# Row constants split over two engines, one batch masked straight from PSUM, and a later start for the second batch's attention

## The chip, the cores and the metric

One Trainium2 core runs the whole program. The metric is the device time of one execution in microseconds (us), as a median over runs.

## What is computed

Three layers in a row over 4 batches of 576 tokens. The first is attention with 8 heads of 64, in which a score stays only if it lies within `tau` of its row's largest:

```python
scores = scale * q @ k.T
thresh = max(scores, -1) - tau
scores = where(scores >= thresh, scores, -1e9)
attn = exp(scores - max) / (sum + 1e-9);  x = attn @ v      # (2304, 512)
h = x @ moe_w_in                                            # (2304, 2048)
g = (a0 + a1 h + a2 h^2 + a3 h^3) / (1 + |b0||h| + |b1| h^2 + 1e-6)
x = g @ moe_w_out                                           # (2304, 512)
h = x @ moe2_w_in
g = where(h >= 1, h, where(h <= -1, 0, (h + 1)^2 / 4))
out = g @ moe2_w_out
```

## The kernel before

The program calls the layer with the rational function MoE1 and the one with the quadratic MoE2. Values are split into a high and a low fp16 part, so that each product of two matrices takes three fp16 products.

**Attention.** A batch has four head pairs, each with nine rows, 36 rows in all. A row is 128 queries (or the last 64 of both heads) against 576 keys. For a row TensorE (PE) makes the scores in a PSUM tile (`scores`), VectorE (DVE) copies them to an SBUF tile `sc` and takes their maximum `mx` in the same instruction (L406), one DVE instruction makes two numbers of each query from `mx`, `nt[:, 0:1]` the threshold and `nt[:, 1:2]` the bias of the exponential (L407), ScalarE (ACT) makes the exponential `e` (L367), DVE masks it against the threshold (L368), ACT and GpSimd (POOL) split it into `hl` (L376 to L378), a DMA transposes that to `eT` (L380), and PE multiplies with `v` (L393). `con` holds the constants of a pair. In batch 0 the rows use two PSUM tiles in turn, tag "s" and the tag "acc" that belongs to the MoE later; in the other batches "s" alone. `prep_v` and `prep_pair` load and split a batch's v and a pair's q and k.

**MoE.** Each of the layers takes 24 steps a batch: three blocks of 192 tokens by eight chunks of 256 hidden columns. A step is a first product (`ph`, L636), the function on DVE, ACT and POOL, and a second product into `acc` (L650).

**Weights.** They come as doubles. A half chunk is loaded as words into a tile with the tag "rw" (two buffers, L219), put together to fp32 by three DVE instructions (L206 to L208), scaled by its power of two and split. MoE1's 16 halves are made beside batch 0's attention, MoE2's 16 halves beside MoE1 of batch 0. The v of batches 1 to 3 is loaded into the same "rw" buffers (L282, L284). After its last half, a maximum over all chunks (`f_max`, L238) is taken, on which the constants of MoE2 hang.

**Order.** A list scheduler sets the order of instructions on each engine from priorities (`at`). The program is written as 192 MoE steps; `spread` puts the pieces of a later batch's attention beside the steps of a range (`ATTENTION`), and the weights' halves beside steps 0 to 20 (`WEIGHTS`). Engines work their queues in order. SP issues all DMAs in one order too, and an issue whose data or buffer isn't ready holds up those behind it.

Of the kernel before, what the change touches and what calls it, by code (L numbers as in the profile page):

```python
# [9 lines left out]
F32 = mybir.dt.float32  # L10
I32 = mybir.dt.int32
AF = mybir.ActivationFunctionType
ALU = mybir.AluOpType
AX = mybir.AxisListType
# [5 lines left out]
LARGEST = 3e38  # L20
LEAST = 2.0**-60
TOP = 2.0**14
LN_E = 6.931471805599453
# [5 lines left out]
N_TEMP, N_POLY, N_WT, N_WH, N_GG, N_ROW, N_SC = 5, 3, 3, 2, 4, 3, 2  # L29


ATTENTION = {1: (14, 50), 2: (60, 100), 3: (108, 147)}
WEIGHTS = (0, 20)


# [1 line left out]
def tile_attention_moe_moe2(  # L37
# [18 lines left out]
    V, A, G, T, Q = nc.vector, nc.scalar, nc.gpsimd, nc.tensor, nc.sync  # L56
    B, H, S, D = q.shape
    P = 128
# [19 lines left out]
    ap = ctx.enter_context(tc.tile_pool(name="ap", bufs=2))  # L78
    xp = ctx.enter_context(tc.tile_pool(name="xp", bufs=1))
    mp = ctx.enter_context(tc.tile_pool(name="mp", bufs=2))  # L80
    sp = ctx.enter_context(tc.tile_pool(name="sp", bufs=4))
# [9 lines left out]
    def small(n, name, keep=False):  # L91
        if keep:
            return cp.tile([P, n], F32, name=name)
        tag = "".join(x for x in name if x.isalpha() or x == "_").rstrip("_")
        return sp.tile([P, n], F32, name=name, tag=f"s{n}_{tag}", bufs=4 if tag in ("mx", "nt") else 2)
# [12 lines left out]
    tau8, tlow = small(1, "tau8", True), small(1, "tlow", True)  # L108
# [22 lines left out]
    V.tensor_scalar(lc[:, 0:1], babs[:, 1:2], LEAST, None, op0=ALU.max)  # L131
    G.memset(lc[:, 1:2], 1.0 + 1e-6)
    A.activation(lc[:, 2:3], lc[:, 0:1], AF.Ln)
    V.tensor_scalar(pc, a_t, binv[:, 1:2], -1.0, op0=ALU.mult, op1=ALU.mult)

    def power(name, src, n, keep=False):


        f, s = small(n, name + "_f", keep), small(n, name + "_s", keep)
        V.tensor_scalar(f, src, 1.0 / TOP, TINY / TOP, op0=ALU.mult, op1=ALU.max)  # L140
        V.tensor_scalar(f.bitcast(I32), f.bitcast(I32), 0x7F800000, None, op0=ALU.bitwise_and)
        V.reciprocal(s, f)
        return f, s

    def root(name, f, src, n=1, even=False):


        s = small(n, name + "_s")
        V.tensor_scalar(f.bitcast(I32), src.bitcast(I32), 1, 0x3F000000 if even else 0x3F800000,
                        op0=ALU.logical_shift_right, op1=ALU.bitwise_and)  # L150
        top = TOP / 2 if even else TOP
        V.tensor_scalar(f, f, 2.0**96 / top, (2.0 if even else 1.0) * TINY / top, op0=ALU.mult, op1=ALU.max)
        V.reciprocal(s, f)
        return s
# [5 lines left out]
    def everywhere(name, src, n, keep=False, place=None):  # L160


        r = small(n, name, keep)
        if place is None:
            place = ps_1.tile([P, 512], F32, name="pm" + name, tag="aux")
        pm = place[:, 0 : n * P].rearrange("p (n q) -> p n q", n=n)
        for i in range(n):
            T.matmul(pm[:, i], src[:, i : i + 1].to_broadcast([P, P]), ident, start=True, stop=True)
        V.tensor_reduce(r, pm, axis=AX.X, op=ALU.max)
        return r  # L170
# [15 lines left out]
    def split(hi, lo, src, scale=None, on_vector=True):  # L186

        if scale is None:
            A.copy(hi, src)  # L189
            G.tensor_tensor(lo, src, hi, op=ALU.subtract)  # L190
        elif on_vector:
            A.activation(hi, src, AF.Copy, scale=scale)
            V.scalar_tensor_tensor(lo, src, scale, hi, op0=ALU.mult, op1=ALU.subtract)
        else:
            A.activation(src, src, AF.Copy, scale=scale)
            split(hi, lo, src)
# [68 lines left out]
    def whole(x):  # L265
        return x[..., 0 : NT * P, :].rearrange("h (p t) d -> p h (t d)", t=NT)
# [34 lines left out]
    def prep_pair(b, pr, on_vector):  # L301
        raws = rp.tile([P, 2, C + 1, D], F32, name=f"rqk{b}_{pr}", tag="rqk", bufs=1)
        raw = raws[:, :, 0:C, :]
        for x, src in enumerate((q, k)):
            Q.dma_start(raws[:, x].rearrange("p (a c) d -> p a (c d)", a=2)[:, :, 0 : NT * D],
                        whole(src[b, 2 * pr : 2 * pr + 2]))
            for ab in range(2):
                Q.dma_start(raw[ab * ST : (ab + 1) * ST, x, NT, :], src[b, 2 * pr + ab, NT * P :, :])
        mx = small(2, f"mqk{b}_{pr}")
        qk = ap.tile([P, 2, C, 2 * D], F16, name=f"qk{b}_{pr}", tag="qk", bufs=1)  # L310
        if b == 0:
            for x in range(2):
                A.activation(qk[:, x, :, 0:D], raw[:, x], AF.Square, scale=2.0**-32, accum_out=mx[:, x : x + 1])
            f = small(2, f"qkf{b}_{pr}")
            s = root(f"qkr{b}_{pr}", f, everywhere(f"mqke{b}_{pr}", mx, 2), 2)
        else:
            V.tensor_reduce(mx, raw.rearrange("p x c d -> p x (c d)"), axis=AX.X, op=ALU.max, apply_absolute_value=True)
            f, s = power(f"qk{b}_{pr}", everywhere(f"mqke{b}_{pr}", mx, 2), 2)

        con = sp.tile([P, 5], F32, name=f"con{b}_{pr}", tag="con", bufs=3)  # L320
        G.memset(con[:, 1:2], 1.0)
        G.memset(con[:, 4:5], LN_E)
        V.scalar_tensor_tensor(con[:, 0:1], f[:, 0:1], cflag, f[:, 1:2], op0=ALU.mult, op1=ALU.mult)
        V.tensor_scalar(con[:, 2:3], con[:, 0:1], -1.0, None, op0=ALU.mult)
        V.scalar_tensor_tensor(con[:, 3:4], s[:, 0:1], tau8, s[:, 1:2], op0=ALU.mult, op1=ALU.mult)
        V.tensor_tensor(con[:, 3:4], con[:, 3:4], tlow, op=ALU.min)
        for x in range(2):
            split(qk[:, x, :, 0:D], qk[:, x, :, D : 2 * D], raw[:, x], s[:, x : x + 1], on_vector)
        qkT = ap.tile([P, 2 * C, P], F16, name=f"qkT{b}_{pr}", tag="qkT")
        Q.dma_start_transpose(out=qkT, in_=qk.rearrange("p x c d -> p (x c d)"))  # L330
        kT2 = ap.tile([P, C, P], F16, name=f"kT2{b}_{pr}", tag="kT2")
        Q.dma_start(kT2[0:D], qkT[D : 2 * D, C : 2 * C, :])
        Q.dma_start(kT2[D : 2 * D], qkT[0:D, C : 2 * C, :])
        return con, qkT, kT2
# [48 lines left out]
    def weighted(pv, rows, eT, cols, vv, h, ab):  # L383

        his, los = [(c, c) for c in range(NT)], [(NT + 1 + c, c) for c in range(NT)]
        if ab:
            his, los = los, his
        blocks = []
        for c, x in [(NT, NT)] + his:
            blocks += [(c, x, 0, D + 1), (c, x, D + 1, D)]  # L390
        blocks += [(c, x, 0, D + 1) for c, x in los]
        for n, (c, x, at, w) in enumerate(blocks):
            T.matmul(pv[rows, 0:w], eT[:, c, cols], vv[:, h * NT + x if x < NT else H * NT + h, at : at + w], start=(n == 0), stop=(n == len(blocks) - 1))  # L393

    def att_rows(b, pr, g, data, pvs):

        con, qkT, kT2, vv, h = data
        name = f"{b}_{pr}_{g}"
        rows = ROWS[3 * g : 3 * g + 3]
        for r, (t, ab) in enumerate(rows):  # L400
            other = b == 0 and r % 2 == 1
            banks = ps_2.tile([P, 1024], F32, name=f"s{name}_{r}", tag="acc" if other else "s")
            scores(banks, t, ab, qkT, kT2)
            mx, nt = small(1, f"mx{name}_{r}"), small(2, f"nt{name}_{r}")
            s = ap.tile([P, S], F32, name=f"sc{name}_{r}", tag="sc", bufs=N_SC)
            V.tensor_scalar(s, banks[:, 0:S], 1.0, -LARGEST, op0=ALU.mult, op1=ALU.max, accum_out=mx)  # L406
            V.scalar_tensor_tensor(nt, con[:, 1:3], mx, con[:, 3:5], op0=ALU.mult, op1=ALU.add)  # L407
            eT = softmax(b, s, ab, con, nt[:, 1:2], nt[:, 0:1], f"{name}_{r}")
            if ab == 0:
                pv = ps_1.tile([P, 512], F32, name=f"pv{b}_{pr}_{t}", tag="ph" if b == 0 else "pv", bufs=2 if b == 0 else 1)  # L410
                pvs[t] = pv[:, 0 : 2 * (2 * D + 2)].rearrange("p (a d) -> p a d", a=2)
            if t < NT:
                weighted(pvs[t][:, ab], slice(0, P), eT, slice(0, P), vv, h + ab, ab)
            else:
                for i in range(2):
                    c = slice(i * ST, (i + 1) * ST)
                    weighted(pvs[t][:, 0], c, eT, c, vv, h + i, 0)
            if ab == 1 or t == NT:
                normalize(b, pr, t, pvs.pop(t))
# [257 lines left out]

    for b, (first, last) in ATTENTION.items():
        spread(first, last, [("att", b)] * N_UNITS)
# [71 lines left out]
```

## Time and profile before

| | us |
|---|---|
| median of three runs | 1337.6 (1337.43 to 1340.25) |
| the profiled execution's own time | 1340.14 |
| its span in the profile | 1338.3 |
| attention of batch 0 and MoE1's weights | 0 to 226.3 |
| MoE1 of batch 0, until its last second product | 226.3 to 389.4 |
| until the first second product of MoE2 | 389.4 to 461.7 |
| MoE2 of batch 0 from there on | 461.7 to 601.8 |
| MoE1 and MoE2 of batch 1 | 605.0 to 871.7 |
| MoE2 of batch 3, the last stage | 1248.1 to 1331.5 |

The stages are cut at the first and last matmuls of L636 and L650 in the trace. An engine's busy share is over the whole span and mixes stages that have different limits. The granted TensorE clock is 0.893 of full on average.

### The profile page before, as it was taken

Reading aid. Unit: us, or ns where it says so; the run is one execution under the profiler, and the core shown is the slowest. Engines: PE = TensorE matmul, PEld = TensorE weight load, DVE = VectorE, ACT = ScalarE, POOL = GpSimd, SP = SyncE. Lnnn points to the kernel's source line nnn. Section 1 sums busy time; section 2 is a strip of 40 time slices with the busy share of each in tenths; the row PEclk is TensorE's granted clock in tenths of the full one; section 3 lists DMA queues with packets and bytes.
Section 4 is the critical chain, followed back from the end, with each engine's and each line's share of the span. In section 5 each row is a group of like instructions: output and inputs, shape, how many; then the busy total and the mean of one; then the engine's idle time right before and its main releaser. Section 6 shows DMA issues by size and latency. Waiting matters only on the chain.

```text
span 1338.3 us, 31403 instructions
## 1 busy us (share of the span) xinstructions
PE 1055.2 (79%) x12498; PEld 962.3 (72%) x12498; DVE 1078.3 (81%) x2497; ACT 796.2 (59%) x1371; POOL 514.2 (38%) x572
## 2 busy tenths in 40 slices
PE   1454355577854589999888999999788998999998
PEld 0233234477752488889877888898778887999998
DVE  6896786899989968778999886889997876898421
ACT  4766554577755546657666565677665565776332
POOL 2764643344324435531135444421353453222221
PEclk9656555798985699999989999999999999999999
DMA  6878785423569737491359564922586539305100
GB/s 200 231 184 209 179 237 162 157 96 111 190 197 257 184 69 126 102 249 45 84 142 217 118 110 73 259 81 45 143 203 131 93 72 240 100 2 184 70 13 25
DMA packets 260275, 187.12 MB, mean 140 GB/s; under 512 B 220960, under 2 KB 233248, under 8 KB 251936
## 3 DMA queue, kind: packets, MB, share of 16 engines
q1 hardware_dynamic: 260128, 185.12, 54.3%
q8 instruction: 98, 1.61, 0.5%
q14 instruction: 49, 0.40, 0.1%
HBM read 106.96 MB, written 21.50 MB: 96 GB/s over the span
## 4 chain that ended last, share of the span: by engine, by line
PE 31%; DVE 28%; DMA 13%; issue 11%; POOL 7%; ACT 6%; SPq 2%; ACTq 0%; DVEq 0%; POOLq 0%
PE acc L650 14%; PE ph L636 13%; DMA eT<-hl 8%; POOL hl L378 4%; DVE e L368 4%; DMA qkT<-qk 3%; DVE sc L406 3%; PE pv L393 2%; DVE wt L207 2%; DVE t L530 2%; DVE t L529 2%; DVE t L523 2%; DVE nt L407 1%; DVE t L528 1%; DVE wt L208 1%
## 5 line engine op out<-in xcount | busy, mean ns | idle before, releaser
L650 PE MATMUL acc<-gg,wc 128*128 128x192 f16 x4608 | 426.2, 247 | 11.4 <-POOL gg L190 6.1
L636 PEld LDWEIGHTS <-wc 128*128 128x128 f16 x4608 | 392.9, 100 | 43.8 <-DVE t L525 24.7
L650 PEld LDWEIGHTS <-wc 128*128 128x128 f16 x4608 | 384.5, 98 | 13.4 <-issue 11.5
L190 POOL TENSOR_TENSOR gg<-t,gg 128x384 f16<-128x384 f32 x192 | 195.1, 1017 | 468.4 <-ACT gg L189 392.8
L636 PE MATMUL ph<-xT,wc 128*128 128x192 f16 x2304 | 221.9, 255 | 32.5 <-DVE t L525 31.1
L636 PE MATMUL ph<-yT,wc 128*128 128x192 f16 x2304 | 219.2, 247 | 2.5 <-DVE t L583 1.9
L378 POOL TENSOR_TENSOR hl<-e,hl 128x512 f16<-128x512 f32 x144 | 177.0, 1229 | 0.0
L367 ACT ACTIVATE e<-sc,nt,con 128x576 f32<-128x576 f32 x144 | 124.0, 865 | 74.5 <-DVE nt L407 62.6
L368 DVE SCALAR_TENSOR_TENSOR e<-sc,nt,e 128x576 f32<-128x576 f32 x144 | 134.7, 936 | 41.0 <-ACT e L367 40.6
L393 PE MATMUL pv<-v,eT 128*128 128x65 f16 (+1 forms) x2240 | 107.0, 207 | 73.8 <-DMA eT<-hl 58.7
L393 PEld LDWEIGHTS <-eT 128*128 128x128 f16 (+1 forms) x2240 | 96.8, 110 | 90.7 <-DMA eT<-hl 68.9
L189 ACT CAST gg<-t 128x384 f16<-128x384 f32 x192 | 97.2, 508 | 90.5 <-DVE t L583 48.2
L357 PE MATMUL s<-qkT 128*128 128x512 f16 (+3 forms) x320 | 95.7, 331 | 65.8 <-DVE sc L406 47.0
L376 ACT CAST hl<-e 128x576 f16<-128x576 f32 x144 | 96.4, 670 | 81.1 <-DVE e L368 66.5
L377 POOL TENSOR_TENSOR hl<-e,hl 128x64 f16<-128x64 f32 x144 | 57.9, 402 | 222.6 <-ACT hl L376 198.6
L582 DVE SCALAR_TENSOR_TENSOR t<-t,c 128x384 f32<-128x384 f32 x96 | 68.7, 716 | 67.2 <-ACT t L581 67.1
L406 DVE TENSOR_SCALAR_CACHE_REDUCE sc<-s 128x576 f32<-128x576 f32 x144 | 107.5, 747 | 14.1 <-PE s L358 13.2
L526 ACT ACTIVATE t<-t,lc 128x384 f32<-128x384 f32 x96 | 67.9, 708 | 44.4 <-DVE t L523 44.1
L521 ACT ACTIVATE t<-ph,sc 128x384 f32<-128x384 f32 x96 | 55.3, 576 | 64.1 <-PE ph L636 63.9
L581 ACT ACTIVATE t<-ph,c 128x384 f32<-128x384 f32 x96 | 63.9, 667 | 47.1 <-PE ph L636 45.3
L358 PEld LDWEIGHTS <-qkT 128*128 128x128 f16 (+1 forms) x320 | 32.3, 111 | 73.3 <-issue 54.5
L358 PE MATMUL s<-kT,qkT 128*128 128x512 f16 (+2 forms) x320 | 76.6, 330 | 5.4 <-DMA kT<-qkT 5.3
(169 smaller groups left out, 1556.2 us busy)
## 6 DMA issues: line engine op xcount, KB each, us to landing
wc<-scratch SPq DMA_DIRECT2D x56, 1024.0 KB, 5.8
rw<-in_moe_w_in_dram SPq DMA_DIRECT2D x16, 1024.0 KB, 5.7
rw<-in_moe_w_out_dram SPq DMA_DIRECT2D x16, 1024.0 KB, 5.4
scratch<-wc SPq DMA_DIRECT2D x8, 1024.0 KB, 5.1
scratch<-wh SPq DMA_DIRECT2D x16, 512.0 KB, 2.9
kT<-qkT SPq DMA_DIRECT2D x32, 144.0 KB, 2.5
rqk<-in_q_dram SPq DMA_DIRECT2D x16, 256.0 KB, 3.1
rqk<-in_k_dram SPq DMA_DIRECT2D x16, 256.0 KB, 3.0
```

What stands on the lines that cost most here:

```text
L189: A.copy(hi, src)
L190: G.tensor_tensor(lo, src, hi, op=ALU.subtract)
L357: T.matmul(s[rows, at : at + w], qkT[:, c, cols], k1[:, k0 : k0 + w], start=True, stop=False)
L358: T.matmul(s[rows, at : at + w], qkT[:, c, cols], k2[:, k0 : k0 + w], start=False, stop=True)
L367: A.activation(e, s, AF.Exp, bias=nb, scale=con[:, 0:1])
L368: V.scalar_tensor_tensor(e, s, th, e, op0=ALU.is_ge, op1=ALU.mult)
L376: A.copy(hi, e)
L378: G.tensor_tensor(lo_w, e[:, whole], hi[:, whole], op=ALU.subtract)
L393: T.matmul(pv[rows, 0:w], eT[:, c, cols], vv[:, h * NT + x if x < NT else H * NT + h, at : at + w], start=(n == 0), stop=(n == len(blocks) ...
L406: V.tensor_scalar(s, banks[:, 0:S], 1.0, -LARGEST, op0=ALU.mult, op1=ALU.max, accum_out=mx)
L636: last = T.matmul(ph[:, f, :], w[:, wx, kt, f * P : (f + 1) * P], rhs, start=(n == 0), stop=(n == 3 * KT - 1))
L650: T.matmul(dst, w[:, wx, f, d * P : (d + 1) * P], gg[:, gx, f, :], start=(i == 0 and f == 0 and n == 0 and d % 2 == 0), stop=(i == NCH - 1 ...
```

## The change

Three edits. First, `con` loses its two fixed columns; the bias becomes an ACT instruction of 128x1 (Identity, with a scale and a bias from SBUF), and the threshold a DVE `tensor_scalar` of 128x1. Second, in batch 0 the scores are not copied: DVE takes their maximum by a reduction, and the exponential and the mask read PSUM. Third, the 17 pieces of batch 1's attention are spread over steps 18 to 50 and no longer 14 to 50.

```diff
-ATTENTION = {1: (14, 50), 2: (60, 100), 3: (108, 147)}
+ATTENTION = {1: (18, 50), 2: (60, 100), 3: (108, 147)}
...
+    ln_e = small(1, "ln_e", True)
+    G.memset(ln_e, LN_E)
...
-        con = sp.tile([P, 5], F32, name=f"con{b}_{pr}", tag="con", bufs=3)
-        G.memset(con[:, 1:2], 1.0)
-        G.memset(con[:, 4:5], LN_E)
+        con = sp.tile([P, 3], F32, name=f"con{b}_{pr}", tag="con", bufs=3)
...
-            s = ap.tile([P, S], F32, name=f"sc{name}_{r}", tag="sc", bufs=N_SC)
-            V.tensor_scalar(s, banks[:, 0:S], 1.0, -LARGEST, op0=ALU.mult, op1=ALU.max, accum_out=mx)
-            V.scalar_tensor_tensor(nt, con[:, 1:3], mx, con[:, 3:5], op0=ALU.mult, op1=ALU.add)
+            if b == 0:
+                s = banks[:, 0:S]
+                V.tensor_reduce(mx, s, axis=AX.X, op=ALU.max)
+            else:
+                s = ap.tile([P, S], F32, name=f"sc{name}_{r}", tag="sc", bufs=N_SC)
+                V.tensor_scalar(s, banks[:, 0:S], 1.0, -LARGEST, op0=ALU.mult, op1=ALU.max, accum_out=mx)
+            A.activation(nt[:, 1:2], mx, AF.Identity, bias=ln_e, scale=con[:, 1:2])
+            V.tensor_scalar(nt[:, 0:1], mx, con[:, 2:3], None, op0=ALU.add)
```

How the order moves is shown at two places. Line numbers of the changed kernel are 2 higher from L131 to L319, the same from L323 to L404, and 5 higher behind the change in `att_rows`. There L407 is batch 0's maximum, L411 the bias on ACT, L412 the threshold, and L368 the mask still.

On DVE, in the second group of rows of batch 0's first pair (names end in pair, group and row, and in a number of their own), weights and norms in between left out, before:

```order
L407 SCALAR_TENSOR_TENSOR nt0_0_1_0_481<-con0_0_162,mx0_0_1_0_480 128x2
L406 TENSOR_SCALAR sc0_0_1_1_526,mx0_0_1_1_524<-s0_0_1_1_519 128x576
L407 SCALAR_TENSOR_TENSOR nt0_0_1_1_525<-con0_0_162,mx0_0_1_1_524 128x2
L368 SCALAR_TENSOR_TENSOR e0_0_1_0_485<-sc0_0_1_0_482,nt0_0_1_0_481,e0_0_1_0_485 128x576
L406 TENSOR_SCALAR sc0_0_1_2_560,mx0_0_1_2_558<-s0_0_1_2_553 128x576
L407 SCALAR_TENSOR_TENSOR nt0_0_1_2_559<-con0_0_162,mx0_0_1_2_558 128x2
L368 SCALAR_TENSOR_TENSOR e0_0_1_1_529<-sc0_0_1_1_526,nt0_0_1_1_525,e0_0_1_1_529 128x576
L406 TENSOR_SCALAR sc0_0_2_0_690,mx0_0_2_0_688<-s0_0_2_0_683 128x576
L407 SCALAR_TENSOR_TENSOR nt0_0_2_0_689<-con0_0_162,mx0_0_2_0_688 128x2
L368 SCALAR_TENSOR_TENSOR e0_0_1_2_563<-sc0_0_1_2_560,nt0_0_1_2_559,e0_0_1_2_563 128x576
```

and now:

```order
L407 TENSOR_REDUCE mx0_0_1_0_478<-s0_0_1_0_473 128x1
L407 TENSOR_REDUCE mx0_0_1_1_522<-s0_0_1_1_517 128x1
L412 TENSOR_SCALAR nt0_0_1_0_479<-mx0_0_1_0_478,con0_0_164 128x1
L412 TENSOR_SCALAR nt0_0_1_1_523<-mx0_0_1_1_522,con0_0_164 128x1
L368 SCALAR_TENSOR_TENSOR e0_0_1_0_483<-s0_0_1_0_473,nt0_0_1_0_479,e0_0_1_0_483 128x576
L368 SCALAR_TENSOR_TENSOR e0_0_1_1_527<-s0_0_1_1_517,nt0_0_1_1_523,e0_0_1_1_527 128x576
L407 TENSOR_REDUCE mx0_0_1_2_556<-s0_0_1_2_551 128x1
```

Before, the copy of a row came ahead of the mask of the row before it, and needed only an `sc` buffer. Now two maxima and two thresholds come first, then two masks, and the maximum of the next row comes behind the mask that gives its PSUM tile back. On ACT the two biases stand ahead of the two exponentials, and the exponentials read `s`:

```order
L411 ACTIVATE nt0_0_1_0_479<-mx0_0_1_0_478,ln_e_121,con0_0_164 128x1
L411 ACTIVATE nt0_0_1_1_523<-mx0_0_1_1_522,ln_e_121,con0_0_164 128x1
L367 ACTIVATE e0_0_1_0_483<-s0_0_1_0_473,nt0_0_1_0_479,con0_0_164 128x576
L367 ACTIVATE e0_0_1_1_527<-s0_0_1_1_517,nt0_0_1_1_523,con0_0_164 128x576
```

No bias waits for DVE's threshold, and both take their row's `mx` alone.

The second place is SP's queue at the end of MoE1 of batch 0, where the last three halves of MoE2's weights (`rw1_6_1`, `rw1_7_0`, `rw1_7_1`) and batch 1's v (`rv1_0`, `rv1_1`) take turns on the "rw" buffers, before (loads of chunks, and of q and k, left out):

```order
L256 DMA wc1_2_4188<-scratch1_123 128x4096
L284 DMA rv1_0_3600<-in_v_dram 128x8x256
L282 DMA rv1_1_3603<-in_v_dram 64x8x64 x2
L249 DMA scratch1_123<-wh1_5_0_3244 128x2048
L330 DMA_TRANSPOSE qkT1_0_3445<-qk1_0_3422 128x18x128
L219 DMA rw1_6_1_3631<-in_moe2_w_out_dram 128x2x1024
L219 DMA rw1_7_0_3716<-in_moe2_w_in_dram 128x4x512
L249 DMA scratch1_123<-wh1_6_0_3514 128x2048
L380 DMA_TRANSPOSE eT1_0_0_0_4031<-hl1_0_0_0_4027 128x9x128
L219 DMA rw1_7_1_3859<-in_moe2_w_out_dram 128x2x1024
```

and now:

```order
L258 DMA wc1_2_4031<-scratch1_125 128x4096
L221 DMA rw1_6_1_3558<-in_moe2_w_out_dram 128x2x1024
L221 DMA rw1_7_0_3643<-in_moe2_w_in_dram 128x4x512
L251 DMA scratch1_125<-wh1_5_0_3238 128x2048
L251 DMA scratch1_125<-wh1_5_1_3323 128x2048
L221 DMA rw1_7_1_3781<-in_moe2_w_out_dram 128x2x1024
L258 DMA wc1_5_4403<-scratch1_125 128x4096
L286 DMA rv1_0_3871<-in_v_dram 128x8x256
L251 DMA scratch1_125<-wh1_6_0_3472 128x2048
L251 DMA scratch1_125<-wh1_6_1_3557 128x2048
```

Before, the v of batch 1 came ahead of the three halves, a pair's transpose (`qkT1_0`) too, and a first row's (`eT1_0_0_0`) stood between them. Now all three halves come ahead of v, and the first row's transpose stands some 20 issues behind.

## Rows read from the trace of the kernel before

**Rows 1.** The page, part 1: busy us of each engine, share, instructions.

```profile
PE 1055.2 (79%) x12498; PEld 962.3 (72%) x12498; DVE 1078.3 (81%) x2497; ACT 796.2 (59%) x1371; POOL 514.2 (38%) x572
```

**Rows 2.** Busy us (x instructions) of each engine by stretch; PEclk; DMA share; GB/s.

```profile
226.30:389.40 163.10, 120.44 (x1238) 113.17 (x1237) 151.01 (x285) 108.80 (x178) 59.69 (x38) 0.89 0.43 149
389.40:461.70 72.30, 29.76 (x235) 20.39 (x236) 66.81 (x194) 39.07 (x64) 27.74 (x30) 0.60 0.85 224
461.70:601.80 140.10, 130.65 (x1750) 120.72 (x1749) 101.16 (x257) 80.80 (x146) 62.97 (x84) 0.99 0.62 135
742.10:871.70 129.60, 121.53 (x1622) 112.53 (x1622) 101.96 (x249) 74.88 (x133) 57.87 (x76) 1.00 0.67 140
1248.10:1331.50 83.40, 83.37 (x1006) 83.09 (x1003) 26.20 (x51) 26.59 (x47) 18.28 (x20) 1.00 0.04 11
```

**Rows 3.** The same for L650 alone: second products in the stretch.

```profile
389.40:461.70 72.30, 0.00 (x0) 0.00 (x1) 0.60 0.85 224
```

**Rows 4.** The same for L368 alone: masks, one for each row.

```profile
389.40:461.70 72.30, 11.62 (x11) 0.60 0.85 224
461.70:601.80 140.10, 22.06 (x25) 0.99 0.62 135
742.10:871.70 129.60, 20.48 (x24) 1.00 0.67 140
```

**Rows 5.** The chain of waits from 30 to 235 us, shares by line.

```profile
by line: issue 18.8%; DVE e L368 8.1%; POOL hl L378 7.7%; DMA eT<-hl 7.1%; DVE sc L406 6.2%; DMA qkT<-qk 5.8%; DVE wt L207 4.9%; DVE wt L208 4.2%; DVE nt L407 3.5%; POOL hl L377 3.3%; POOL wc L190 3.0%; DVE wt L206 3.0%; ACT wt L195 2.4%; A
```

**Rows 6.** Groups by line, 0 to 226.3 us: busy us, mean ns; idle before, releasers.

```profile
L407 DVE SCALAR_TENSOR_TENSOR nt<-con,mx 128x2 f32<-128x2 f32 x36 | 20.9, 584 | 0.2
...
L368 DVE SCALAR_TENSOR_TENSOR e<-sc,nt,e 128x576 f32<-128x576 f32 x36 | 37.3, 1039 | 5.8 <-ACT e L367 5.8
...
L357 PE MATMUL s<-qkT 128*128 128x512 f16 (+3 forms) x80 | 29.2, 413 | 43.4 <-DVE sc L406 31.5 <-DMA qkT<-qk 11.7
```

**Rows 7.** Line L407: ns min/median/max, first and last start; who waited.

```profile
L407 DVE SCALAR_TENSOR_TENSOR nt<-con,mx x144: 195/222/2118, 39.2 to 1128.4; 128x2 f32<-128x2 f32 x144
...
  ACT e L367: 62.6, 66
```

**Rows 8.** Line L406, the same columns.

```profile
L406 DVE TENSOR_SCALAR_CACHE_REDUCE sc<-s x144: 727/746/759, 37.9 to 1127.4; 128x576 f32<-128x576 f32 x144
L406 DVE DVE_READ_ACCUMULATOR sc<-s x144: 73/80/85, 38.6 to 1128.1; 128x1 f32 x144
```

**Rows 9.** Line L368, the same columns.

```profile
L368 DVE SCALAR_TENSOR_TENSOR e<-sc,nt,e x144: 792/817/2599, 42.2 to 1130.3; 128x576 f32<-128x576 f32 x144
```

**Rows 10.** Line L407 by stretch: DVE busy us (x instructions).

```profile
742.10:871.70 129.60, 8.44 (x24) 1.00 0.67 140
```

**Rows 11.** Line L553, a 128x1 `tensor_scalar` with an SBUF scalar.

```profile
L553 DVE TENSOR_SCALAR iv<-fy,iy x12: 197/202/212, 322.9 to 1247.8; 128x1 f32<-128x1 f32 x12
```

**Rows 12.** Line L140, a `tensor_scalar` of 128x2 in SBUF.

```profile
L140 DVE TENSOR_SCALAR qk_f<-mqke x12: 138/344/1136, 383.6 to 1036.8; 128x2 f32<-128x2 f32 x12
```

**Rows 13.** Line L523, two tensors in SBUF.

```profile
L523 DVE SCALAR_TENSOR_TENSOR t<-t,qc x96: 592/612/2167, 231.6 to 1225.8; 128x384 f32<-128x384 f32 x96
```

**Rows 14.** Line L583, the same width, one tensor in PSUM.

```profile
L583 DVE SCALAR_TENSOR_TENSOR t<-ph,c,t x96: 589/616/619, 454.1 to 1323.1; 128x384 f32<-128x384 f32 x96
```

**Rows 15.** Line L595, a maximum over PSUM.

```profile
L595 DVE TENSOR_REDUCE my<-acc x12: 941/948/958, 308.1 to 1243.1; 128x1 f32<-128x768 f32 x12
```

**Rows 16.** Line L558, an ACT instruction of 128x1.

```profile
L558 ACT ACTIVATE g<-g x12: 186/198/208, 435.9 to 1249.7; 128x1 f32<-128x1 f32 x12
```

**Rows 17.** SP's timeline: start us, length, line, out<-in.

```profile
368.34 0.38 SPq L284 DMA_DIRECT2D rv<-in_v_dram  x1
...
402.70 0.37 SPq L219 DMA_DIRECT2D rw<-in_moe_w_out_dram  x1
...
413.09 0.37 SPq L219 DMA_DIRECT2D rw<-in_moe_w_out_dram  x1
```

**Rows 18.** DVE's timeline: the last maximum over MoE2's weights.

```profile
440.14 0.14 DVE L238 TENSOR_REDUCE f_max<-f_w 128x1 f32<-128x8 f32 x1
```

More of the change, by code (lines that the diff above doesn't have):

```diff
@@ L318, in prep_pair @@
             f, s = power(f"qk{b}_{pr}", everywhere(f"mqke{b}_{pr}", mx, 2), 2)
-        con = sp.tile([P, 5], F32, name=f"con{b}_{pr}", tag="con", bufs=3)
-        G.memset(con[:, 1:2], 1.0)
-        G.memset(con[:, 4:5], LN_E)
+        con = sp.tile([P, 3], F32, name=f"con{b}_{pr}", tag="con", bufs=3)
         V.scalar_tensor_tensor(con[:, 0:1], f[:, 0:1], cflag, f[:, 1:2], op0=ALU.mult, op1=ALU.mult)
-        V.tensor_scalar(con[:, 2:3], con[:, 0:1], -1.0, None, op0=ALU.mult)
-        V.scalar_tensor_tensor(con[:, 3:4], s[:, 0:1], tau8, s[:, 1:2], op0=ALU.mult, op1=ALU.mult)
-        V.tensor_tensor(con[:, 3:4], con[:, 3:4], tlow, op=ALU.min)
+        V.tensor_scalar(con[:, 1:2], con[:, 0:1], -1.0, None, op0=ALU.mult)
+        V.scalar_tensor_tensor(con[:, 2:3], s[:, 0:1], tau8, s[:, 1:2], op0=ALU.mult, op1=ALU.mult)
+        V.tensor_tensor(con[:, 2:3], con[:, 2:3], tlow, op=ALU.min)
         for x in range(2):
```

## The prediction

> **What bounds the kernel now.** I read the busy shares first: DVE and PE lead with 81% and 79% [rows 1], so neither bounds all of it, and the stages have to be read apart. By stretch [rows 2] the last stage, MoE2 with no attention beside it, is PE alone: 83.37 of 83.4 us. MoE2 of batch 1 with 24 rows beside it [rows 4] takes 129.6 us, PE 94% busy, so a row costs (129.6 - 83.4)/24 = 1.93 us of stage. MoE2 of batch 0 takes 140.1 us with 25 rows, 2.27 us a row. These are stages of PE with DVE at 70 to 80%. Two others aren't. From 389.4 to 461.7 PE does no second product at all [rows 3] while DVE is 92% busy: the last weight halves are being made, with 11 rows among them [rows 2, 4]. And up to 226 us, batch 0's attention beside MoE1's weights, the chain of waits runs over many things, none above a fifth [rows 5]; of what the change touches, the mask (8.1%), the copy with its maximum (6.2%) and `nt` (3.5%) lie on it.
>
> **Edit one and two up to 226 us.** `nt` takes 584 ns in the mean there [rows 6], where its shortest is 195 and its longest 2118 [rows 7]. The new threshold is a 128x1 `tensor_scalar` with an SBUF scalar; such a one takes 202 ns and at most 212 [rows 11]. So DVE saves 0.38 us a row. The copy takes 746 ns and an accumulator read of 80 [rows 8]. A maximum over 768 PSUM columns takes 948 [rows 15]; scaled by width, 576 take 711, and as part of it is fixed I take 746, so that only the 80 ns go. The mask takes 1039 ns in the mean [rows 6], 817 in the median and 792 at best [rows 9]. How long one that reads PSUM takes, no row shows; the nearest are two operations of one width, with both tensors in SBUF 612 in the median and 2167 at most [rows 13], with one in PSUM 616 and never above 619 [rows 14]. So I take 817, with bounds of 616 x 576/384 = 924 and 792: 0.22 us a row (0.12 to 0.25). In sum 0.68 us x 36 rows = 24.6 us of DVE.
>
> What of it counts goes by the chain [rows 5], which is 205 us long: `nt` has 7.2 us, of which (584 - 202)/584 go, 4.7; the mask 16.6, of which 222/1039 go, 3.5; the copy 12.7, of which 80/826 go, 1.2. Together 9.4 us; I take 9, with nothing and 24.6 as bounds. ACT gets 36 instructions of 128x1, some 0.2 us each [rows 16], 7 us in 226; each stands before its row's exponential and takes the place of a longer `nt` there, so I charge nothing. If ACT were the limit, it would cost these 7 us. The memsets that go were POOL's, outside the rows' path.
>
> [...]
>
> **Edit two's wait.** A PSUM tile was free once its copy ended; now it is held until the mask's end, and the next row's score products on that tile, and the maximum behind them in DVE's queue, wait for that. The first row's copy begins at 37.9 us [rows 8] and its mask at 42.2 [rows 9]; with 0.8 of mask that is 5.1 us, to which come the score products, some 0.8 us for each of the two lines [rows 6], so a tile turns in 6.7 us and with two tiles a row can come each 3.4 us. The stage needs one each (226.3 - 37.9)/36 = 5.2 us. I charge nothing for it in the sum.
>
> **Edit three.** Before, batch 1's v took a buffer of the weights at 368.34, and the three halves behind it went out at 402.70, and the last at 413.09 [rows 17]. The last maximum over the weights came at 440.14 [rows 18], 27.0 us behind the last load, and the first second product 21.6 us later. Now the halves come ahead of v. If they move up by as much as the first of them can, 402.70 - 368.34 = 34.4 us, and all behind them stays as long, MoE2 begins at 427.3. But 11 rows also leave that stretch: their masks are 11.62 us [rows 4], copies and `nt` about as much again, up to 24 us of DVE, which was full there. So 403 at best; MoE1's own last product at 389.4 stays ahead of it. I take the middle, 415.
>
> These rows aren't gone, they fall into MoE2: 36 there and not 25. By 2.27 us a row the stage takes 83.4 + 36 x 2.27 = 165 us, by 1.93 153. DVE's need there, by (101.96 - 26.20)/24 = 3.16 us a row [rows 2], is 26 + 114 = 140 us, which fits in. I take the former rate, since it is this stage's own: it ends at 580 and not at 601.8, a gain of 22. The 46 us that the gap gives are halved by the rows that it hid. Bounds: 403 + 153 = 556 (46 gained) and 427 + 165 = 592 (10 gained).
>
> **After 602 us** 72 rows remain. `nt` takes 8.44/24 = 352 ns there [rows 10], so DVE saves 0.15 x 72 = 11 us in stages that PE bounds to 94%. I take a third, 4, with nothing and 11 as bounds.
>
> **The sum** against the profiled execution's 1340.1: 9 + 22 + 4 = 35, so 1305.1. That execution lies 2.5 above the median of 1337.6, so the median should become 1302.6, say 1303.
>
> **The rivals.**
> *MoE2 of batch 0 gives the gap back.* All 36 rows with the preparation of v and the pairs now fall on it, and its DVE and POOL work with them. For it speaks that this stage already took 2.27 a row where the later took 1.93; against it that DVE's 140 fit in 165. The third edit's gain is gone at (601.8 - 415 - 83.4)/36 = 2.87 us a row. At 2.75 the stage ends at 597 and 4 are left: 1320.
> *The first two edits do nothing.* The threshold could still wait as `nt` did: a `tensor_scalar` two wide in SBUF took up to 1136 ns [rows 12], though the one-wide never [rows 11], and the mask's excess could come from elsewhere. Then only 22 are left: 1316. [...]
> *All of it counts.* DVE gives its 24.6 whole up to 226 us, and MoE2 runs at 1.93 a row, ending at 568 (34): 1340.1 - 62.6 - 2.5 = 1275. For it speaks that DVE was full in the gap; against it that the chain puts much on DMAs and issue.
> *Held score tiles, slower.* If a maximum, an exponential and a mask are queued behind conversions of 1.4 us a piece on DVE, a tile is held for longer than the first row's. The stage lengthens once a tile turns in over 10.4 us (two tiles at 5.2 a row), and the whole is slower than before beyond 5.2 + 26/36 = 5.9 a row, a turn of 11.8 us, when the other 26 are eaten too. At 6.4 a row it costs 43: 1340.1 + 43 - 26 - 2.5 = 1355. Against it stands the first row's 6.7.
>
> **Chances.** The forecast 0.40; the gap given back 0.20; no effect of the first two 0.14; all of it 0.14; held tiles 0.12. About 0.2%, 2.7 us, is what a measurement of this kernel tells from no change. Faster gets the forecast, the second and third rival and four fifths of the first, 0.84; the same 0.04; slower the last, 0.12. The range goes from 1274, which takes in most of "all of it", to 1334, the weakest case in which the gap is mostly given back; the slower case stays outside.
>
> **What would show it.** In the new profile the threshold near 0.2 us and never over 0.25, the mask up to 226 us near 0.82, the first product after that near 217 and not 226. No stretch of over 30 us without second products behind MoE1 of batch 0; the first of MoE2 near 415 less the shift of the stage before; MoE2 of batch 0 at 36 masks and some 165 us. I would be wrong if score products up to 226 us wait mostly for the mask, if that stage doesn't begin to end earlier although DVE's work falls, or if MoE2 of batch 0 shows DVE above 95% and PE far below.

## The result, and the profile after

The median fell from 1338.9 us (four runs; 1337.6 was that of the first three) to 1325.4 (1324.86 to 1325.63, four runs), a ratio of 0.9892 with a 95% interval of 0.9866 to 0.9919. That is 14 us of the 35 forecast: the sign was right, the size wrong by more than half.

By stretch of the changed kernel, with the columns of [rows 2]: up to MoE1's first product, from MoE1's last second product in batch 0 to MoE2's first, MoE2 of batch 0 from there, and MoE2 of batch 1.

```profile
0.00:219.40 219.40, 102.09 (x850) 65.79 (x851) 164.86 (x373) 139.17 (x243) 116.15 (x112) 0.72 0.78 208
381.60:424.50 42.90, 11.56 (x69) 9.14 (x69) 34.13 (x105) 21.81 (x38) 11.22 (x7) 0.56 0.64 202
424.50:591.50 167.00, 149.06 (x1921) 133.75 (x1919) 139.66 (x356) 109.18 (x209) 80.52 (x99) 0.96 0.73 154
721.80:860.10 138.30, 128.17 (x1692) 117.88 (x1691) 103.20 (x267) 88.80 (x168) 60.85 (x74) 1.00 0.66 141
```

The start is 6.9 us shorter (219.4 for 226.3). MoE1 gives another 0.9. The gap fell from 72.3 to 42.9 us, but MoE2 of batch 0 grew from 140.1 to 167.0 [rows 2], with all 36 masks in it, so that the two together gave only 212.4 - 209.9 = 2.5 us. What follows gave 5. In sum the profiled execution's own time fell by 15 us, from 1340.14 to 1324.86.

The instructions of a row, as ns min/median/max, answer to [rows 7 to 9]:

```profile
L411 ACT ACTIVATE nt<-mx,ln_e,con x144: 371/386/391, 40.7 to 1112.7; 128x1 f32<-128x1 f32 x144
L412 DVE TENSOR_SCALAR nt<-mx,con x144: 186/205/219, 37.6 to 1113.3; 128x1 f32<-128x1 f32 x144
L367 ACT ACTIVATE e<-sc,nt,con x108: 853/867/873, 427.9 to 1114.0; 128x576 f32<-128x576 f32 x108
L367 ACT ACTIVATE e<-s,nt,con x36: 809/830/833, 41.9 to 197.8; 128x576 f32<-128x576 f32 x36
L368 DVE SCALAR_TENSOR_TENSOR e<-sc,nt,e x108: 794/818/1564, 430.2 to 1115.3; 128x576 f32<-128x576 f32 x108
...
L368 DVE SCALAR_TENSOR_TENSOR e<-s,nt,e x36: 792/807/819, 42.9 to 201.1; 128x576 f32<-128x576 f32 x36
```

The threshold takes 205 ns and never over 219, and the mask from PSUM 807 and never over 819: both as forecast. The bias on ACT takes 386 in the median, not the 198 that I read from another 128x1 instruction [rows 16]. The exponential that reads PSUM (830 ns) is 37 ns shorter than the one that reads SBUF (867).

SP's timeline, answering to [rows 17]: the three last halves (`rw`) and behind them batch 1's v (`rv`).

```profile
361.80 0.38 SPq L221 DMA_DIRECT2D rw<-in_moe_w_out_dram  x1
...
368.37 0.38 SPq L221 DMA_DIRECT2D rw<-in_moe_w_in_dram  x1
...
384.42 0.38 SPq L221 DMA_DIRECT2D rw<-in_moe_w_out_dram  x1
...
388.48 0.38 SPq L286 DMA_DIRECT2D rv<-in_v_dram  x1
```

The halves now go out ahead of v, but spread over 22.6 us, where before it was 10.4. There are two "rw" buffers, so the last half has to wait until the first of the three has been converted and gives its buffer back. What SP's queue waited for from 372 to 390 us (us, times, longest), and that conversion on DVE (start us, length, instruction, in brackets the idle time before it and what ended it):

```profile
SPq L221 <- DVE wt L210: 1.9, 1, 1.9
```

```profile
378.68 1.39 DVE L208 TENSOR_SCALAR wt<-rw 128x1024 int32<-128x1024 int32 x1 [3.44 <-POOL wh L192]
380.10 3.03 DVE L209 SCALAR_TENSOR_TENSOR wt<-rw,wt 128x1024 int32<-128x1024 int32 x1
383.17 1.23 DVE L210 SCALAR_TENSOR_TENSOR wt<-rw,wt 128x1024 int32<-128x1024 int32 x1
```

The half that went out at 361.80 is converted from 378.68 on, behind a wait of 3.4 us for POOL, and done at 384.40. The last load goes out at 384.42. DVE and PE behind that:

```profile
396.94 2.29 DVE L287 TENSOR_REDUCE mv<-rv 128x1 f32<-128x2048 f32 x1 [4.64 <-DMA rv<-in_v_dram]
399.14 0.68 DVE L208 TENSOR_SCALAR wt<-rw 128x1024 int32<-128x1024 int32 x1
...
406.19 0.14 DVE L240 TENSOR_REDUCE f_max<-f_w 128x1 f32<-128x8 f32 x1
```

```profile
417.99 0.61 PE L357 MATMUL s<-qkT 128*128 128x512 f16 x1 [4.68 <-DMA qkT<-qk]
...
424.52 0.25 PE L655 MATMUL acc<-gg,wc 128*128 128x192 f16 x1
```

Here stand two waits for attention's preparation, ahead of the weights or of MoE2's first steps. DVE waits 4.6 us for v's DMA and then takes 2.3 for its maximum, and the conversion of the last half stands behind that in its queue; the last maximum over the weights comes at 406.19. PE waits 4.7 us for the first pair's transpose (`qkT`), ahead of MoE2's first products in its queue. The first second product is at 424.52.

### The profile page after: what moved, and what is told of

Same layout as the page of the kernel before. It is cut to its first block, busy times and chain, and to the rows that moved or that the text cites. A ratio compares the mean times of both kernels' runs of the same rounds, so it can differ in the third digit from the quotient of the medians.

```text
span 1323.1 us, 31559 instructions
## 1 busy us (share of the span) xinstructions
PE 1056.3 (80%) x12498; PEld 961.1 (73%) x12498; DVE 1050.1 (79%) x2461; ACT 839.3 (63%) x1515; POOL 515.6 (39%) x541
## 4 chain that ended last, share of the span: by engine, by line
DVE 31%; PE 26%; DMA 12%; issue 11%; ACT 8%; POOL 7%; SPq 2%; DVEq 0%; POOLq 0%; ACTq 0%
PE acc L655 12%; PE ph L641 11%; DMA eT<-hl 7%; DVE e L368 4%; POOL hl L378 3%; DVE wt L209 2%; DMA qkT<-qk 2%; DVE sc L410 2%; DMA rqk<-in_k_dram 2%; DVE t L534 2%; DVE t L535 2%; PE pv L393 2%; DVE t L533 2%; DVE t L587 2%; POOL gg L192 2%
## 5 line engine op out<-in xcount | busy, mean ns | idle before, releaser
L192 POOL TENSOR_TENSOR gg<-t,gg 128x384 f16<-128x384 f32 x192 | 197.9, 1031 | 476.1 <-ACT gg L191 382.3
L378 POOL TENSOR_TENSOR hl<-e,hl 128x512 f16<-128x512 f32 x144 | 173.5, 1205 | 0.0
L393 PEld LDWEIGHTS <-eT 128*128 128x128 f16 (+1 forms) x2240 | 94.1, 109 | 84.0 <-DMA eT<-hl 71.4
L377 POOL TENSOR_TENSOR hl<-e,hl 128x64 f16<-128x64 f32 x144 | 62.4, 433 | 198.8 <-ACT hl L376 198.4
L357 PE MATMUL s<-qkT 128*128 128x512 f16 (+2 forms) x320 | 94.8, 326 | 45.6 <-DVE e L368 17.8
L587 DVE SCALAR_TENSOR_TENSOR t<-t,c 128x384 f32<-128x384 f32 x96 | 71.6, 746 | 67.9 <-ACT t L586 67.8
L368 DVE SCALAR_TENSOR_TENSOR e<-sc,nt,e 128x576 f32<-128x576 f32 x108 | 97.4, 902 | 29.2 <-ACT e L367 28.9
L367 ACT ACTIVATE e<-sc,nt,con 128x576 f32<-128x576 f32 x108 | 93.5, 866 | 6.6 <-POOL hl L378 0.2
L411 ACT ACTIVATE nt<-mx,ln_e,con 128x1 f32<-128x1 f32 x144 | 55.2, 384 | 55.1 <-DVE sc L410 44.7
L410 DVE TENSOR_SCALAR_CACHE_REDUCE sc<-s 128x576 f32<-128x576 f32 x108 | 80.9, 749 | 10.8 <-PE s L358 10.4
```

The source lines that it names most:

```text
L357: T.matmul(s[rows, at : at + w], qkT[:, c, cols], k1[:, k0 : k0 + w], start=True, stop=False)
L367: A.activation(e, s, AF.Exp, bias=nb, scale=con[:, 0:1])
L368: V.scalar_tensor_tensor(e, s, th, e, op0=ALU.is_ge, op1=ALU.mult)
L378: G.tensor_tensor(lo_w, e[:, whole], hi[:, whole], op=ALU.subtract)
L587: V.scalar_tensor_tensor(u, u, top, u, op0=ALU.min, op1=ALU.mult)
```

## Experiments

Each ratio is against runs of the kernel before on the same chip, with its 95% interval. Five kernels were measured twice, in different groups of runs and on different chips, and their two ratios lay 0.1 to 0.4 points apart (the changed kernel's 0.9892 and 0.9849, for one). So a difference of up to 0.4 points, some 5 us, between kernels that were not measured beside each other shows nothing.

### Each edit alone, and in pairs

First the third edit alone, and the first two without it:

```diff
-ATTENTION = {1: (14, 50), 2: (60, 100), 3: (108, 147)}
+ATTENTION = {1: (18, 50), 2: (60, 100), 3: (108, 147)}
```

> The third edit alone, on the kernel before. In the changed kernel the time from MoE1's last second product to MoE2's last one in batch 0 fell only from 212.4 to 209.9 us. If the edits are separable, this kernel is 1 to 4 us faster than before, with its first second product of MoE2 35 to 40 us earlier than before and MoE2 of batch 0 some 25 us longer. If the three edits depend on each other (the rows of batch 1, costing less on DVE, are what lets the later start pay), it is as slow as before or slower. The forecast on record would have it 22 us faster.

> The first two edits with batch 1's attention left at step 14. If the edits are separable, 10 to 13 us faster than before: 7 up to the first product of MoE1 (226.3 to 219.4 us), the rest of it in the stages behind MoE2 of batch 0. If they depend on each other, less than 7 in sum, since what they gain early is waited away at the weights.

The third alone: 0.991 (0.9883 to 0.9937). The first two: 0.9907 (0.9882 to 0.9932). The third gave 12 us where 1 to 4 were expected. Either nearly gives what all three gave in the first measurement, so they don't seem to add up. Then the first alone and the second alone, on another chip:

```diff
-            V.scalar_tensor_tensor(nt, con[:, 1:3], mx, con[:, 3:5], op0=ALU.mult, op1=ALU.add)
+            A.activation(nt[:, 1:2], mx, AF.Identity, bias=ln_e, scale=con[:, 1:2])
+            V.tensor_scalar(nt[:, 0:1], mx, con[:, 2:3], None, op0=ALU.add)
...
```

```diff
+            if b == 0:
+                s = banks[:, 0:S]
+                V.tensor_reduce(mx, s, axis=AX.X, op=ALU.max)
...
```

> The first edit alone on the kernel before (bias on ACT, threshold on DVE; batch 0 still copied, start 14). The first two edits together gave 0.9907. If what DVE's long two-tensor instruction cost was the point, this alone gives about half of that or more: 5 to 9 us faster, with 3 to 5 us of it up to MoE1's first product. If the ACT instruction of 384 ns that the exponential now waits for takes it back, it is 0 to 3 us faster, and the gain of the first two was the second's.

> The second edit alone on the kernel before (batch 0 masked from PSUM, bias and threshold by the one two-wide DVE instruction). If the mask without waits is what shortens the start, MoE1's first product comes 3 to 6 us earlier than at 226.3 and the total falls by 3 to 6 us. If score tiles held until the mask's end cost as much as the faster mask saves, the total stays within 2 us of before.

The first alone 0.9894 (0.9871 to 0.9916), the second alone 0.9959 (0.9942 to 0.9975). The first gave 14 us where 5 to 9 were expected, and is worth as much alone as with the second. MoE1's first product came at 216.9 with the first, 222.7 with the second and 219.4 with both: on top of the first, the second costs 2.5 us there. What PE waited for before its score products up to that time, with the first alone, in the changed kernel, and with the second alone:

```profile
L357 PE MATMUL s<-qkT 128*128 128x512 f16 (+3 forms) x80 | 28.2, 397 | 24.1 <-DVE sc L406 14.2 <-DMA qkT<-qk 9.7
```

```profile
L357 PE MATMUL s<-qkT 128*128 128x512 f16 (+3 forms) x80 | 30.3, 430 | 31.6 <-DVE e L368 17.8 <-DVE f_w L151 4.5 <-DMA qkT<-qk 3.6
```

```profile
L357 PE MATMUL s<-qkT 128*128 128x512 f16 (+3 forms) x80 | 29.5, 417 | 36.8 <-DVE e L368 28.6 <-DMA qkT<-qk 6.0 <-DVE f_w L149 1.9
```

From the first alone to the changed kernel, the wait for a copy (14.2 us) has become one for a mask (17.8). That the held tile is what costs the 2.5 us is read from these waits and not tested: with the second edit alone PE waits even longer for the mask there (28.6 us), and the first product still comes 3.6 us earlier than before. The pairs that were missing, beside the changed kernel on one chip:

> The first and the third edit without the second (batch 0's scores copied). If these two add up, 0.9804 of before, 26 us faster, and it is the second edit that spoils the sum. If the ACT instruction lengthens the packed MoE2 of batch 0, which is 167 us in the changed kernel and 157 with the third edit alone, the two don't add up and this is 0.986 to 0.991, no better than either alone.

> The second and the third edit without the first. If these add up, 0.987 of before, with MoE2 of batch 0 at some 157 us as with the third alone, and MoE1's first product near 222.7. If it is the held score tiles that spoil the sum, it is no better than the third alone, 0.991.

> The changed kernel once more: 0.987 to 0.992 of before, as on the first chip.

The first and third: 0.9785 (0.9765 to 0.9805). The second and third: 0.9811 (0.979 to 0.9833). All three: 0.9849 (0.9821 to 0.9876). So the second edit, added to the other two, costs 0.6 points, some 9 us, and the intervals are apart. The first, added to the other two, costs 0.4 points, and there the intervals overlap. The second and third together are better than the sum that was expected (0.987). It is the three together that go badly, and not the second edit by itself. Whether first and third add up was still a matter of different chips:

> The third edit alone, beside the first alone and both together. On another chip it was 0.991. If chips differ as the changed kernel's two measurements did, it is 0.987 to 0.991 here.

> The first edit alone, 0.9894 on another chip; 0.985 to 0.990 here.

> The first and third together, 0.9785 on another chip. If the two add up, the distance from 1 is the sum of the two distances measured beside it, within 0.3 points. If they share what they gain, it falls short of the sum by 0.5 points or more.

The third 0.9873 (0.9847 to 0.9899), the first 0.9907 (0.9879 to 0.9934), both 0.9774 (0.9749 to 0.98). The distances are 1.27 and 0.93 points, in sum 2.20, and together they have 2.26: they add up.

Where the second edit's 9 us go is seen in the stretches. On one chip, from the profile with the first and third edits to that of the changed kernel beside it, the span grows by 8.2 us (1313.5 to 1321.7): 2.9 up to MoE1's first product (216.0 to 218.9) and 5.6 from MoE1's last second product to MoE2's last (200.9 to 206.5). In the two other profiles of the same two kernels the latter difference is 10.6. The kernel with the first and third edits, from MoE1's last second product to MoE2's last, and MoE2 of batch 0 alone:

```profile
377.20:576.50 199.30, 152.56 (x1987) 136.80 (x1988) 172.90 (x460) 131.62 (x246) 91.45 (x106) 0.91 0.73 172
419.60:576.50 156.90, 141.07 (x1922) 127.69 (x1920) 138.13 (x356) 109.87 (x208) 80.30 (x99) 1.00 0.76 163
```

In the changed kernel these are 209.9 and 167.0 us. PE has 1921 matmuls in the second there and 1922 here, and takes 149.06 us for them and not 141.07, at a granted clock of 0.96 and not 1.00: 8.0 of the 10.1 us. The changed kernel's waits from 515 to 545 us (what waited for what: us, times, longest) and its windows show the place where the largest piece of it falls:

```profile
ACT gg L191 <- PE acc L655: 4.9, 1, 4.9
...
PE pv L393 <- DMA eT<-hl: 3.7, 2, 3.3
```

```profile
534.66:541.40 6.74, 6.74 (x52) 6.16 (x53) 2.79 (x8) 2.59 (x5) 0.91 (x1) 0.54 0.59 128
```

ACT waits 4.9 us for a second product to give a `gg` buffer back, PE waits 3.3 us for the transpose of a row, and then runs for 6.7 us at a granted clock of 0.54. In that time 24 matmuls of MoE2's first products took 3.87 us (537.36 to 541.24, clock 0.54), where 17 took 1.56 shortly before (from 527.34, clock 1.00): 161 and 92 ns each. At the full clock the work of the 6.7 us would take some 3.6, by an estimate of 6.74 x 0.54 that lets its time go as the clock, so wait and clock together are at most 6.4 of the 10.1 us. The second profile of the changed kernel has the same dip (0.83 from 525 to 545 us). No instruction of the second edit runs there. But the order of the instructions is another: the traces list PE's instructions of this stretch in the same order in both profiles of one kernel, and in a different one in the two kernels. That this order is what costs the time was seen, not tested.

### The ACT instruction

```diff
-            A.activation(nt[:, 1:2], mx, AF.Identity, bias=ln_e, scale=con[:, 1:2])
+            V.tensor_scalar(nt[:, 1:2], mx, con[:, 1:2], LN_E, op0=ALU.mult, op1=ALU.add)
```

> The changed kernel with the bias too as a 128x1 tensor_scalar on DVE, so that a row has two such instructions of 0.2 us and none on ACT. On ACT the bias took 384 ns and the exponential waits for it. If the row's path counts, the exponential starts 0.2 us earlier a row and ACT is freed of 55 us: 3 to 8 us faster than the changed kernel. If DVE's work counts, its 144 further instructions of 0.2 us, 29 us, cost more than that: 3 to 10 us slower.

> The kernel with the bias on DVE once more, beside the changed kernel on the same chip. If the ACT instruction costs what the first measurement said, it is 6 to 10 us faster than the changed kernel; if that was chance, the two are within 3 us.

0.984 (0.9811 to 0.9869), and again, beside the changed kernel with 0.9849 (0.9821 to 0.9876), 0.9796 (0.9773 to 0.982): 7 us faster than the changed kernel, with intervals that just miss each other. It adds 144 instructions of 0.2 us to DVE and is still faster. MoE2 of batch 0 took 161.3 and 158.7 us in the two profiles, in the changed kernel 167.0 and 164.2. But the same without the second edit failed:

> The changed kernel with bias and threshold both as 128x1 instructions on DVE and without the second edit (batch 0's scores copied to SBUF as before). If the second edit adds to the others, this is 3 to 8 us slower than the kernel with the bias on DVE and the PSUM mask (0.984 of before). If the tiles held until the mask's end eat what the faster mask saves, it is within 3 us of that one.

0.994 (0.9918 to 0.9961), with runs from 1325.7 to 1336.9. It is 1.0 and 1.4 points slower than the kernel with the PSUM mask, and some 1.6 slower than the first and third edits with the bias on ACT, more than two chips have differed by. MoE1's last second product comes at 389.2 there, 5.5 us later than with the PSUM mask. So the bias on DVE isn't better in itself: it is better beside the second edit, and worse without it; and the second edit is a loss with the bias on ACT and a gain with it on DVE. Neither of the theories stated foresaw this.

### What holds up MoE2's start

```diff
...
+            with tc.issue_after(f_ins[1, 1]) if b == 1 else nullcontext():
-            V.tensor_reduce(mx[:, g : g + 1], raw.rearrange("p t d -> p (t d)"), axis=AX.X, op=ALU.max,
-                            apply_absolute_value=True)
+                V.tensor_reduce(mx[:, g : g + 1], raw.rearrange("p t d -> p (t d)"), axis=AX.X, op=ALU.max,
+                                apply_absolute_value=True)
```

> The changed kernel, with the maxima over batch 1's v put in DVE's queue behind the last maximum over the weights. In the changed kernel the first of them stands ahead of the last half's conversion and waits 4.6 us for v's DMA, then takes 2.3. Theory of the queues: the late start of MoE2 (424.5 us) comes of attention's preparations that stand ahead of the weights and of the first functions and wait for their DMAs; then the last maximum over the weights comes some 7 us earlier than at 406.2, and MoE2 begins 3 to 7 us earlier, the total falls by 2 to 7. Theory of the work: the halves' own conversion (DVE, ACT, POOL) is the limit; then neither moves by more than 2 us, total within 2 us of the changed kernel.

0.9844 (0.9814 to 0.9873), which lies by the changed kernel's 0.9849 and 6 us below its 0.9892, so that a gain isn't shown. The last maximum over the weights came at 402.7, 3.4 us earlier and not 7, and MoE2 began at 427.1, 2.6 later and not 3 to 7 earlier. The theory of the queues fails here for MoE2's start. PE's timeline shows what it waited for:

```profile
414.26 0.61 PE L359 MATMUL s<-qkT 128*128 128x512 f16 x1 [4.06 <-DMA qkT<-qk]
417.87 0.61 PE L360 MATMUL s<-kT,qkT 128*128 128x512 f16 x1 [3.01 <-DMA kT<-qkT]
```

The transpose again, and then the transfer behind it (`kT`): 4.1 and 3.0 us. So the next experiment put the preparation of pairs and v behind MoE2's first function on DVE and ACT, and the first score products behind the first second product:

```diff
-ATTENTION = {1: (18, 50), 2: (60, 100), 3: (108, 147)}
+ATTENTION = {1: (26, 50), 2: (60, 100), 3: (108, 147)}
...
+                with at(t - 1.5), ExitStack() as pins:
+                    if u[1] == 1:
+                        for e in ("DVE", "ACT") if taken[0] < 3 else ("PE",):
+                            pins.enter_context(tc.issue_after(firsts[e]))
+                        taken[0] += 1
```

> The changed kernel with batch 1's attention at steps 26 to 50, and the DVE and ACT work of its first three pieces (first pair, v, second pair) queued behind the function of MoE2's first step, and its first score products behind the first second product. In the changed kernel PE waits 4.7 us for the first pair's transpose at 413 to 418, and ACT and DVE split q, k and v between the constants and the first function. Theory of the queues: MoE2 then begins at 412 to 417 and not at 424.5. If the rows then go at the same 2.3 us each, MoE2 of batch 0 ends 5 to 10 us earlier and the total falls by 5 to 10. Rival: the rows that come later still lengthen that stage, or hold up MoE1 of batch 1, by as much, and the total stays within 3 us of the changed kernel, or is slower. Theory of the work: MoE2 begins within 2 us of 424.5.

0.9884 (0.9858 to 0.9911), between the changed kernel's two ratios. MoE2 begins at 420.2, 4.3 us earlier and not 7 to 12, so the queues were a small part of the delay. Yet it ends at 594.4, 3 us later, with rows that now begin at 432.2 and not 418.0. This is as the rival has it: an earlier start is given back by later rows. The two changes that had lower ratios than the changed kernel, together:

> The changed kernel with both changes that each beat it: bias on DVE (0.984 of before) and v's maxima behind the weights' (0.9844). If they act on different waits, it is 14 to 17 us faster than the changed kernel, 0.977 to 0.980 of before. If both do the same (a different order of the same rows beside MoE2), it is no better than 0.983.

0.9845 (0.982 to 0.9871), no better than either (0.984 and 0.9844).

### What bounds MoE2 of batch 0

The first of two kernels leaves out the mask of batch 1, the second one of three fp16 products in the second products of MoE2 of batch 0.

```diff
+        if b != 1:
-        V.scalar_tensor_tensor(e, s, th, e, op0=ALU.is_ge, op1=ALU.mult)
+            V.scalar_tensor_tensor(e, s, th, e, op0=ALU.is_ge, op1=ALU.mult)
...
+                    if (m, b, n) == (1, 0, 1):
+                        continue
...
```

> The changed kernel without the 36 masks of batch 1 (left out: the threshold of that batch's scores), 36 us less work on DVE between MoE1 and the end of MoE2 of batch 0, where DVE is 83% busy and PE 77%. MoE2's last second product came there 209.9 us behind MoE1's. If DVE's work sets this stretch, it becomes 20 to 30 us shorter. If PE's order and the DMAs of the rows set it, or the time that MoE2 begins, it becomes 0 to 8 us shorter. My forecast (PE's work, 2.3 us a row from the first second product on) has less than 8.

> The changed kernel with two and not three fp16 products in the second products of MoE2 of batch 0 (left out: the low part of the hidden values of that batch), 192 matmuls of 0.25 us, some 19 us (192 x 0.1 us at the issue rate of the last stage at least) less work on PE and none on DVE. If PE's work sets MoE2 of batch 0, as the forecast took it, that stretch becomes 14 to 19 us shorter. If DVE's work, or the rows' own path, sets it, it becomes 0 to 6 us shorter.

Their ratios were 0.9784 (0.9764 to 0.9803) and 0.9791 (0.9772 to 0.9811). The stretch from MoE1's last second product to MoE2's last, in the changed kernel, without the masks, and with two products:

```profile
381.60:591.50 209.90, 160.62 (x1987) 142.89 (x1987) 173.79 (x460) 130.99 (x247) 91.74 (x106) 0.88 0.71 164
```

```profile
383.70:578.00 194.30, 153.06 (x1988) 137.58 (x1987) 140.41 (x424) 130.40 (x245) 85.34 (x104) 0.90 0.75 175
```

```profile
382.75:577.60 194.85, 142.90 (x1763) 123.85 (x1762) 167.37 (x445) 127.60 (x238) 91.25 (x103) 0.87 0.76 175
```

209.9 us became 194.3 with DVE's busy time down from 173.8 to 140.4, and 194.9 with PE's down from 160.6 to 142.9. Taking 33 us from DVE gives 15.6, taking 18 from PE gives 15.0; against the changed kernel's second profile, with 206.5, it is 12.2 and 11.7. So both hold the stretch, and neither of the stated theories alone was right. Which holds it more isn't told: both kernels are scheduled anew, and without the masks PE's busy time too falls by 7.6 us (160.62 to 153.06) for as many matmuls, at a granted clock of 0.90 and not 0.88.

## Why the prediction was right or wrong, step by step

By stages, 19.7 of the 35 us are missing, and 19.5 of them between MoE1 of batch 0 and the end of MoE2 of batch 0, where 22 were forecast and 2.5 came.

**Up to 226 us.** 9 forecast, 6.9 measured. The durations of threshold and mask were right. The first edit alone brought MoE1's first product to 216.9, 9.4 earlier, where the sum had 4.7 for it; the second alone 3.6, where it had 4.7. The step that failed is "I charge nothing for it", on the score tile that is held: on top of the first, the second edit costs 2.5 us here. PE's score products then wait most for the mask (17.8 of 31.6 us), which the forecast itself named as a sign of being wrong. The tile's turn was not mis-sized: from the start of a row's maximum to the end of its mask it is 5.2 us in the median of the 36 rows, where 5.1 was taken. What was wrong was to take such a wait as free because the tiles turn fast enough on the mean; how it comes to cost 2.5 us stays open.

**The ACT instruction.** Mis-sized: 386 ns in the median and not 0.2 us. The instruction that I took [rows 16] has its scale as a number in the instruction and no bias from SBUF, and in the changed kernel it takes 198 (L563) as before. It also computes another function (Ln, where the bias is an Identity), and no run changes one of these things alone, so which of them makes the 188 ns isn't shown. In the sum it stood at nothing. With the second edit in place, moving it to DVE gave 7 us.

**MoE2's start.** This is the step that failed most: "If they move up by as much as the first of them can, ... and all behind them stays as long". I had the start near 415 less the shift of the stages before it (8), so at 407; it came at 424.5, 17 us later. The shift of 34 us that I gave the loads held for the first only (361.80, or 40.9 earlier, of which 8 are the shift of the stages before). The last came 28.7 earlier, so it is 13.5 us later than I had it. It waits for one of two buffers, and so for the conversion of the half that went out first, which DVE ended at 384.40. The other 4 us lie behind that load: of the 48.6 us there 40 stayed, where I took the half of 11 rows' DVE work off. DVE is busy for 34 of the 42.9 us without second products, and of the two waits that were moved out of the way one brought the start no gain and the other 4.3 us, so the rest of these 40 us stays open. The late start is the third edit's own: alone it has 42.6 us without second products, from 387.6 to 430.1, and the same three loads spread over 22.6 us (367.76 to 390.36). No kernel with more buffers for the halves was run, so that the buffers are the cause is read from the traces and not tested.

**MoE2's length.** 165 forecast, 167.0 measured, so the rate of 2.27 us a row came out for the changed kernel. That is partly luck: with the third edit alone the 36 rows took 157.0 (430.1 to 587.2), 2.04 a row, and with the first and third 156.9. The rival that has the gap given back was nearest in time (1320), though not by its mechanism, a rate near 2.75.

**The sum.** Of the 35, the first and the third edit had 31 (4.7, 22 and 4), and together they measured 29 to 30. That is luck too: up to MoE1's first product they gave 11.6 (226.3 to 214.7), not 4.7, and the stretch to the end of MoE2 of batch 0 gave 13.1 (212.4 to 199.3), not 22, with a late start and a short MoE2. The second edit had 4.7, and alone it measured 5.5; but on top of the other two it costs 9, and by edits this is the larger part of what is missing. The rest lies within what two measurements of a kernel have differed by. That gains add was the step of the sum that failed. The larger part of the 9 lies in MoE2 of batch 0; only its place was seen, and the cause stays open.

**After 602 us.** 4 forecast, 5.0 measured.

## What to carry to other kernels

Gains that each hold alone need not add up when a scheduler sets the order anew (here the second edit gave 5.5 us alone and cost 9 on top of the other two): try the edits in pairs on one chip before all are kept. When loads take turns on a few buffers, moving the first one up need not move the last by as much (here 40.9 and 28.7 us): follow each load to the work that gives its buffer back before you shift them all by one number. When a stretch has an idle engine, ask what the first instruction behind it waits for in its queue, and then test it, for here the two waits that stood out were worth 0 and 4 us of 17. A shorter instruction that holds a buffer longer has to be priced with the engine that waits for the buffer (here PE, 17.8 us for masks up to MoE1's first product).

## What the runs showed of the hardware

All of these are from the changed kernel. An exponential over 576 columns took 830 ns in the median from PSUM (36 in batch 0) and 867 from SBUF (108 in the other batches). The mask of one PSUM and one SBUF tensor never took above 819 ns in those 36, the same with both in SBUF up to 1564 in the 108; their medians were 807 and 818. An ACT instruction of 128x1 with scale and bias from SBUF took 386 ns, a DVE `tensor_scalar` of 128x1 205.
